# Zero products in sequence on one column strip, and a new order of the start, in a gated mix of two attention branches

## The chip, the cores and the metric

One core of a Trainium2 chip runs the kernel. The metric is the device time of one execution in microseconds; of the kernel before there are three timed runs, and the median counts. The engines are TensorE (matrix products), VectorE, ScalarE, GpSimd and SyncE (it only issues DMAs here); in the views of the profile they are PE (PEld for its weight loads), DVE, ACT, POOL and SP. They run side by side, each through its own queue in order, and wait for each other through semaphores.

## What is computed

x is 1 x 2048 x 512. Two attention branches with 32 heads of 16 read it: full attention (A), and local attention over 8 positions with a step of 2 (B). A gate per row mixes them.

```python
g = _sigmoid((x * gate_w).sum(-1, keepdims=True))
# A: qkv = x @ A_wqkv, per head of 16:
scores = einsum("bhqd,bhkd->bhqk", q, k) * Dh ** -0.5
o = einsum("bhqk,bhkd->bhqd", softmax(scores), v)      # then @ A_wo
# B: the same with 8 keys a row, idx = pos - 2 * [0..7], masked below 0, then @ B_wo
return g * a + (1 - g) * b
```

## The kernel before

Branch A makes the exponentials of 32 heads x 2048 x 2048 scores. The work is cut into **periods**: a chunk of 512 queries and a group of 4 heads (32 periods). A period has 64 **units**, each one head and one tile of 128 keys, so 128 x 512 scores. TensorE multiplies a unit's keys with the chunk's queries (`qk`, L815, tile `ring`), ScalarE takes the exponential (`ex`, L821, tile `pT`), TensorE multiplies it with the values and adds to the period's accumulator (`pv`, L834, tile `acc`). Units go in **sets** of three and two in turn, over two score buffers (`rA`, `rB`) with three `pT` buffers each. The last few units of a period have their exponential made on VectorE by a polynomial (`d_group`, L855: tiles `misc`, `dt`, `dg`, `pd`). The four heads of a group use the four column strips of TensorE's array (32 columns each); products on different strips run together.

A row's scores are shifted ahead of the exponential by a bound: the largest key entry (`kmax`) of a head times the absolute values of the query. For that a group's keys are copied to SBUF with a constant row (`kc`, L443, tile `kt_all`), their largest absolute value is reduced (`km`, L447), the maxima go into `selk_all` (L455), and a period's query projection (`q_proj`, L513) is followed by its copy (`qc`), its absolute value (`ab`), a product with `selk_all` (`bd`) and a sum (`ev`). Only then can the period's scores start.

At the start, x (four chunks of 512 rows) and the weights are loaded by SyncE (L380 to L388), TensorE transposes each chunk in two halves into the PSUM tile `pxt` (`tr`, L402), ScalarE copies the first half to `xT` and VectorE the second (`ev`, L412). Group 0's keys and values are projected, and the first query. Twelve products of constants (`warm`, L391) come first on TensorE.

Branch B (`b_tile`, L610) projects a tile of 128 rows, writes keys and values to DRAM, reads them back shifted, and GpSimd multiplies and adds; 16 tiles, one each 46.7 us from `b_start` in the plan.

The order is that of a **list scheduler** in the kernel's Python (`list_schedule`, L79). Every piece of work is an `Op` with an engine, an estimated duration, a due time, what it depends on and the buffers (`Tok`) it takes. The scheduler simulates the five engines with these estimates, always starts the due-first piece that can start, and the instructions are emitted in the order of the simulated times; each engine runs its own in that order. `S0` (L285) holds the planned start of each period, from `T0` (L265) at 0.457 us a unit. PSUM's `misc` tiles (two) serve all projections, `acc` (one) the accumulator.

The scheduler also keeps TensorE busy: a `pv` step may be preceded by **zero products** (`z32` times `ones_t`, added to the running accumulator, so they change nothing). Before the change a step gets four of them, one for each strip whose accumulation is open (L148 and L835), when the products counted in the last 3.2 us are under 20, or under 12 where the four would make the next scores late:

```python
            if o.fill and have < (DENSE_MIN if w is None or t + occ + FILL <= w[1] else DENSE_LOW):
                o.filled = True
                occ, lat, n = occ + FILL, lat + FILL, n + 4
```

In this count score products have no weight, and each value product counts one.

Of the kernel before, what the change touches and what calls it, by code (L numbers as in the profile page):

```python
# [21 lines left out]
    b_start=32.0,  # L22
# [34 lines left out]
class Op:  # L57

    def __init__(self, eng, occ, fn, dl, deps=(), alloc=(), use=(), lat=None, rel=0.0, name="",
                 dense=0, fill=False, after=(), cls="a"):  # L60
        self.eng, self.occ, self.fn, self.dl, self.rel, self.name = eng, occ, fn, dl, rel, name
        self.dense, self.fill, self.filled = dense, fill, False
# [4 lines left out]
        self.cls, self.clock = cls, False  # L67
# [4 lines left out]
QK_LEAD, LATE, DENSE_LOW = 0.6, 1.0, 12  # L72
LAT = dict(pe=0.25, dve=0.10, act=0.22, pool=2.5, sp=2.2)
DENSE_SPAN, DENSE_MIN, FILL = 3.2, 20, 0.35
# [4 lines left out]
def list_schedule(ops):  # L79
# [48 lines left out]
    while len(out) < len(ops):  # L128
# [19 lines left out]
        if o.dense:  # L148
            recent = [(tr, n) for tr, n in recent if tr > t - DENSE_SPAN]
            n = o.dense  # L150
            have = sum(x[1] for x in recent) + n
            if o.fill and have < (DENSE_MIN if w is None or t + occ + FILL <= w[1] else DENSE_LOW):
                o.filled = True
                occ, lat, n = occ + FILL, lat + FILL, n + 4
            recent.append((t, n))
# [17 lines left out]
def kernel(  # L173
# [91 lines left out]
    T0 = 22.0  # L265
# [51 lines left out]

    def init_dve():
        V.memset(ones_t[:], 1.0)
# [8 lines left out]
        V.memset(z32[:], 0.0)  # L328
# [13 lines left out]
    o_init_d = op("dve", 2.2, init_dve, -9.0)  # L342
# [37 lines left out]
    o_x[0] = op("sp", 0.5, load_x(0), -9.0, alloc=[xtok[0]], lat=5.5)  # L380
    o_wk = op("sp", 0.5, load_w(1), -8.9, lat=6.5)
    o_x[1] = op("sp", 0.5, load_x(1), -8.8, alloc=[xtok[1]], lat=7.5)
    o_x[2] = op("sp", 0.5, load_x(2), -8.7, alloc=[xtok[2]], lat=9.5)
    o_wq = op("sp", 0.5, load_w(0), -8.6, lat=11.0)
    o_x[3] = op("sp", 0.5, load_x(3), -8.5, alloc=[xtok[3]], lat=12.0)
    o_wv = op("sp", 0.5, load_w(2), -8.4, lat=13.0)
    o_bw = op("sp", 1.0, load_bw, -8.3, lat=19.0)
    o_wo = op("sp", 3.5, load_wo, -8.2, deps=[o_wz], lat=24.0)  # L388


    def warm():  # L391
        t_ = misc_ps([128, QW])
        for _ in range(3):
            mm_ct(t_, selq[:], ones_t[:], True, True)
    o_warm = op("pe", 4.0, warm, -9.0, deps=[o_init_d], alloc=[tok("misc", 2)])

    o_xt = []
    for sc in range(NC):
# [22 lines left out]
        t1 = op("pe", 0.6, tr(0), -5.0 + sc, deps=[o_x[sc], o_id], alloc=[tk], use=[xtok[sc]])  # L421
        t2 = op("pe", 0.6, tr(1), -4.9 + sc, deps=[t1], use=[tk, xtok[sc]])
        o_xt.append([op("act", 1.0, ev(0), -5.0 + sc, deps=[t1], use=[tk]),
                     op("dve", 0.68, ev(1), -4.9 + sc, deps=[t2], use=[tk])])
    all_xt = [o for os_ in o_xt for o in os_]


    o_kc = {}
    o_selk = {}

    def k_proj(i, sc, tag, dl, rel=0.0):
# [657 lines left out]
```

## Time and profile before

| what | us |
|---|---|
| median of 3 runs (941.53 to 947.1) | 944.49 |
| the profiled execution | 943.72 |
| its span, first to last instruction | 941.8 |
| first exponential on ScalarE | 25.58 |
| exponentials over 1536 columns, 386, each | 1.57 |
| exponentials over 1024 columns, 387, each | 1.14 |
| zero products, 974, on TensorE | 110.3 busy |

Rows of the profile's groups give engine, operation, what it writes and reads, busy time and mean duration. A product of 512 columns shows some 0.38 us, but products follow each other closer than that, since they are pipelined; so the length of a run of products is read from the timeline, and a busy TensorE is not one at its peak. Lines of a helper stand for many callers here (L230 for all of VectorE, ScalarE, GpSimd and SyncE, L239 for most products), so one goes by the tiles' names. The mean granted clock of TensorE is 0.989.

### The profile page before, as it was taken

What the parts mean: (1) busy time and instruction counts of PE and PEld (TensorE: products, weight loads), DVE (VectorE), ACT (ScalarE), POOL (GpSimd) and SP (SyncE); (2) the same over time, 40 slices, a digit from 0 to 9 for tenths busy, and PEclk for the clock granted to TensorE, in tenths of its full rate; (3) what the DMA queues carried; (4) which work ended last, traced back from release to release, by engine and by line L of the source; (5) the groups of instructions that cost most, each with busy time, mean ns of one, the idle gap of its engine ahead of it and who ended that gap; (6) DMA issues with size and microseconds to landing.
All of it is one profiled execution on the core that took longest, in us unless ns stands there. A gap on an engine that the chain in (4) does not pass through costs nothing.

```text
span 941.8 us, 20153 instructions
## 1 busy us (share of the span) xinstructions
PE 824.4 (88%) x8427; PEld 269.6 (29%) x8427; DVE 703.5 (75%) x877; ACT 888.9 (94%) x795; POOL 709.9 (75%) x540
## 2 busy tenths in 40 slices
PE   7999998888998889988999888888988888788997
PEld 4323233222332323222233222222222222222222
DVE  5587768768687788986253776978888698896776
ACT  2999999999999999999998999989999999899894
POOL 2355969598796999898969894999999999980000
PEclk9999999999999999999999999989999899999999
DMA  9301110203030112013030221130303010100001
GB/s 268 103 2 57 45 58 1 102 1 102 1 102 1 57 46 78 25 57 101 18 108 18 67 68 44 33 101 1 82 21 102 1 46 1 46 1 1 1 6 42
DMA packets 43940, 47.48 MB, mean 50 GB/s; under 512 B 1813, under 2 KB 41285, under 8 KB 43849
## 3 DMA queue, kind: packets, MB, share of 16 engines
q1 hardware_dynamic: 43848, 46.19, 15.5%
q8 instruction: 66, 1.08, 0.5%
q14 instruction: 26, 0.20, 0.1%
HBM read 39.86 MB, written 6.33 MB: 49 GB/s over the span
## 4 chain that ended last, share of the span: by engine, by line
ACT 43%; issue 19%; DVE 19%; PE 14%; POOL 4%; DMA 1%; SPq 0%; DVEq 0%; ACTq 0%; POOLq 0%
ACT pT L230 42%; DVE dg L230 6%; PE acc L239 5%; PE ring L239 4%; POOL prod L230 4%; DVE pd L230 4%; PE misc_ps L239 3%; DVE dt L230 1%; DVE kt_all L230 1%; DVE qt L230 1%; PE misc L239 1%; DVE kmax_all L230 1%; DVE accT L230 1%; DVE ott L230 1%; DVE lg L230 1%
## 5 line engine op out<-in xcount | busy, mean ns | idle before, releaser
L230 ACT ACTIVATE pT<-ring 128x1536 bf16<-128x1536 f32 (+1 forms) x773 | 881.8, 1355 | 25.3 <-PE ring L239 17.4
L239 PE MATMUL ring<-qt,kt_all 32*128 32x512 bf16 x1932 | 307.8, 383 | 82.5 <-ACT pT L230 76.1
L239 PE MATMUL acc<-pT,vp_all 128*17 128x512 bf16 (+1 forms) x1932 | 295.6, 386 | 5.4 <-DVE accT L230 5.2
L230 POOL TENSOR_TENSOR prod<-prod 128x512 f32<-128x512 f32 (+1 forms) x208 | 292.9, 1420 | 6.3
L230 POOL TENSOR_TENSOR prod<-ksh,qb 128x512 f32<-128x512 bf16 x128 | 179.8, 1434 | 71.8 <-issue 39.1
L239 PEld LDWEIGHTS <-kt_all 32*128 32x128 bf16 x2048 | 115.5, 91 | 398.4 <-issue 391.5
L230 POOL TENSOR_TENSOR prod<-vsh,lg 128x512 f32<-128x512 bf16 x128 | 162.9, 1302 | 51.8 <-DVE lg L230 30.5
L230 DVE TENSOR_SCALAR dt<-misc 128x512 f32<-128x512 f32 x116 | 79.7, 687 | 64.8 <-PE misc L239 57.6
L230 DVE SCALAR_TENSOR_TENSOR dg<-dt,dg 128x1024 bf16<-128x1024 uint16 x65 | 110.0, 1693 | 1.8
L239 PE MATMUL acc<-ones_t,z 128*32 128x512 bf16 x974 | 110.3, 393 | 0.0
L230 DVE SCALAR_TENSOR_TENSOR pd<-dg,dt 128x1024 uint16<-128x1024 bf16 x65 | 105.3, 1620 | 1.1
L239 PEld LDWEIGHTS <-vp_all 128*17 128x17 bf16 (+1 forms) x1932 | 70.0, 89 | 100.2 <-issue 90.7
L230 DVE SCALAR_TENSOR_TENSOR dg<-dt 128x1024 bf16<-128x1024 uint16 x65 | 93.6, 1440 | 1.8
L239 PE MATMUL misc_ps<-xT,wst 128*32 128x512 bf16 x1024 | 93.3, 389 | 0.4 <-DVE dt L230 0.3
L239 PE MATMUL misc_ps<-bw,xT 128*32 128x512 bf16 x768 | 69.0, 382 | 0.2 <-DVE vp_all L230 0.2
L239 PE MATMUL misc<-qt,kt_all 32*128 32x512 bf16 x116 | 44.5, 383 | 2.9 <-DVE dt L230 1.4
L239 PE MATMUL misc_ps<-woarr,oat 128*32 128x512 bf16 x512 | 43.7, 382 | 1.0 <-DVE fb L230 0.8
L239 PEld LDWEIGHTS <-z 128*32 128x32 bf16 x974 | 27.1, 93 | 58.1 <-issue 57.1
L239 PEld LDWEIGHTS <-xT 128*32 128x32 bf16 (+1 forms) x1088 | 33.7, 96 | 26.0 <-issue 17.8
L230 DVE CAST kvs<-misc_ps 128x512 bf16<-128x512 f32 x32 | 21.8, 682 | 21.6 <-PE misc_ps L239 21.5
L230 DVE TENSOR_SCALAR kt_all<-misc_ps,rowc 128x512 bf16<-128x512 f32 x32 | 25.6, 801 | 16.4 <-PE misc_ps L239 16.4
L239 PE MATMUL acc<-pd,vd_all 128*17 128x512 bf16 x116 | 28.0, 390 | 9.0 <-DVE pd L230 8.4
(71 smaller groups left out, 524.6 us busy)
## 6 DMA issues: line engine op xcount, KB each, us to landing
ksh<-kv_scr SPq DMA_DIRECT2D x16, 1024.0 KB, 6.2
vsh<-kv_scr SPq DMA_DIRECT2D x16, 1024.0 KB, 9.1
kv_scr<-kvs SPq DMA_DIRECT2D x16, 256.0 KB, 2.0
xld<-in_A_x_dram SPq DMA_DIRECT2D x4, 512.0 KB, 4.9
out_dram<-osb SPq DMA_DIRECT2D x16, 128.0 KB, 1.8
wst<-in_A_wqkv_dram SPq DMA_DIRECT2D x3, 512.0 KB, 4.9
bw<-in_B_wqkv_dram SPq DMA_DIRECT2D x1, 1536.0 KB, 10.2
bwo<-in_B_wo_dram SPq DMA_DIRECT2D x1, 512.0 KB, 14.1
```

Of the source, the lines that this page charges most:

```text
L230: return chain_on(key, f(*a, **k))
L239: return chain(nc.tensor.matmul(out, lhsT=lhsT, rhs=rhs, start=start, stop=stop, **kw))
```

## The change

- **Start.** x's fourth chunk is loaded ahead of the query weights. The two halves of a chunk's transposes follow each other (`after` orders two pieces by their start, without waiting for the end). TensorE's first products are seven on one strip, `z32` times `ones_t`, behind a step with only those two memsets, and one more behind chunk 0's transposes. Group 0's keys are copied by ScalarE (`kc_act`) while VectorE reduces their maxima, now from the PSUM tile itself. Group 0's values are projected after the first query's `bd`. Due times and planned durations of these steps change, and `T0` and `b_start` are earlier.
- **Zero products.** The scheduler counts passes of TensorE: a projection step of eight products two, a value step one, a score step 0.75. Where fewer than 8.6 lie in the last 3.4 us, one or two zero products go ahead of a value step, in sequence on one strip that this step uses (floor 6.8 where they would make scores late). Where TensorE is planned idle for over 0.5 us and the count is low, further ones are put into the gap (`pre`).

```diff
-    b_start=32.0,
+    b_start=26.0,
...
-QK_LEAD, LATE, DENSE_LOW = 0.6, 1.0, 12
+QK_LEAD, LATE, ACTIVE_LOW, GAP_MIN = 0.6, 1.0, 6.8, 0.5
 LAT = dict(pe=0.25, dve=0.10, act=0.22, pool=2.5, sp=2.2)
-DENSE_SPAN, DENSE_MIN, FILL = 3.2, 20, 0.35
+SPAN, ACTIVE, FILL, FILL1 = 3.4, 8.6, 0.25, 0.10
...
-        if o.dense:
-            recent = [(tr, n) for tr, n in recent if tr > t - DENSE_SPAN]
+        if e == "pe":
+            recent = [(tr, n) for tr, n in recent if tr > t - SPAN]
+            act = sum(n for tr, n in recent)
+            idle = t - free[e]
+            if t > 30.0 and idle > GAP_MIN and act < ACTIVE:
+                o.pre = min(int((idle - 0.1) / FILL), int(ACTIVE - act + 1))
+                recent.append((t - 0.1, o.pre))
+                act += o.pre
             n = o.dense
-            have = sum(x[1] for x in recent) + n
-            if o.fill and have < (DENSE_MIN if w is None or t + occ + FILL <= w[1] else DENSE_LOW):
-                o.filled = True
-                occ, lat, n = occ + FILL, lat + FILL, n + 4
+            if o.fill and act + n < ACTIVE:
+                for k in (2, 1):
+                    more = FILL1 + k * FILL
+                    if act + n + k - 1 < ACTIVE and (w is None or t + occ + more <= w[1] or act + n + k - 1 < ACTIVE_LOW):
+                        o.filled = k
+                        occ, lat, n = occ + more, lat + more, n + k
+                        break
...
-    T0 = 22.0
+    T0 = 19.0
...
+    def init_warm():
+        V.memset(z32[:], 0.0)
+        V.memset(ones_t[:], 1.0)
...
-    o_init_d = op("dve", 2.2, init_dve, -9.0)
+    o_init_w = op("dve", 0.6, init_warm, -9.5)
+    o_init_d = op("dve", 1.8, init_dve, -9.0, deps=[o_init_w])
...
-    o_x[0] = op("sp", 0.5, load_x(0), -9.0, alloc=[xtok[0]], lat=5.5)
-    o_wk = op("sp", 0.5, load_w(1), -8.9, lat=6.5)
-    o_x[1] = op("sp", 0.5, load_x(1), -8.8, alloc=[xtok[1]], lat=7.5)
-    o_x[2] = op("sp", 0.5, load_x(2), -8.7, alloc=[xtok[2]], lat=9.5)
-    o_wq = op("sp", 0.5, load_w(0), -8.6, lat=11.0)
-    o_x[3] = op("sp", 0.5, load_x(3), -8.5, alloc=[xtok[3]], lat=12.0)
-    o_wv = op("sp", 0.5, load_w(2), -8.4, lat=13.0)
-    o_bw = op("sp", 1.0, load_bw, -8.3, lat=19.0)
-    o_wo = op("sp", 3.5, load_wo, -8.2, deps=[o_wz], lat=24.0)
-
-
-    def warm():
-        t_ = misc_ps([128, QW])
-        for _ in range(3):
-            mm_ct(t_, selq[:], ones_t[:], True, True)
-    o_warm = op("pe", 4.0, warm, -9.0, deps=[o_init_d], alloc=[tok("misc", 2)])
+    o_x[0] = op("sp", 0.5, load_x(0), -9.0, alloc=[xtok[0]], lat=4.7)
+    o_wk = op("sp", 0.5, load_w(1), -8.9, lat=5.7)
+    o_x[1] = op("sp", 0.5, load_x(1), -8.8, alloc=[xtok[1]], lat=6.7)
+    o_x[2] = op("sp", 0.5, load_x(2), -8.7, alloc=[xtok[2]], lat=7.7)
+    o_x[3] = op("sp", 0.5, load_x(3), -8.6, alloc=[xtok[3]], lat=8.7)
+    o_wq = op("sp", 0.5, load_w(0), -8.5, lat=9.6)
+    o_wv = op("sp", 0.5, load_w(2), -8.4, lat=10.6)
+    o_bw = op("sp", 1.0, load_bw, -8.3, lat=14.5)
+    o_wo = op("sp", 3.5, load_wo, -8.2, deps=[o_wz], lat=17.0)
+
+
+    def warm(n):
+        def s():
+            t_ = misc_ps([128, QW])
+            for _ in range(n):
+                mm(t_[0:32, :], z32[:], ones_t[:], True, True, tile_position=(0, 0))
+        return s
+    op("pe", 3.2, warm(7), -30.0, deps=[o_init_w], alloc=[tok("misc", 2)])
...
-        t1 = op("pe", 0.6, tr(0), -5.0 + sc, deps=[o_x[sc], o_id], alloc=[tk], use=[xtok[sc]])
-        t2 = op("pe", 0.6, tr(1), -4.9 + sc, deps=[t1], use=[tk, xtok[sc]])
-        o_xt.append([op("act", 1.0, ev(0), -5.0 + sc, deps=[t1], use=[tk]),
-                     op("dve", 0.68, ev(1), -4.9 + sc, deps=[t2], use=[tk])])
+        if sc == 1:
+            op("pe", 0.45, warm(1), -21.0, after=[t2], alloc=[tok("misc", 2)])
+        t1 = op("pe", 0.57 if sc else 1.0, tr(0), -20.0 + sc, deps=[o_x[sc], o_id], alloc=[tk], use=[xtok[sc]])
+        t2 = op("pe", 0.57 if sc else 1.0, tr(1), -19.9 + sc, after=[t1], use=[tk, xtok[sc]])
+        o_xt.append([op("act", 1.0, ev(0), -20.0 + sc, deps=[t1], use=[tk]),
+                     op("dve", 0.68, ev(1), -19.9 + sc, deps=[t2], use=[tk])])
...
+        def kc_act():
+            A.activation(out=kt_all[:, i, sc * QW:(sc + 1) * QW], in_=st["pk"][:], func=ACT.Identity,
+                         scale=rowc[:, 0:1], bias=rowc[:, 1:2])
+
         def km():
-            V.tensor_reduce(out=kmax_all[:, i, sc:sc + 1], in_=kt_all[:, i, sc * QW:(sc + 1) * QW],
-                            axis=AX.X, op=ALU.max, apply_absolute_value=True)
-        a = op("pe", WAVE(2), part(0, 2), dl - 2.6, dense=8, deps=[o_wk, o_init_d] + o_xt[sc], alloc=[tk], rel=rel, name=f"kp{i}.{sc}")
-        b = op("pe", WAVE(2), part(2, DC), dl - 2.0, dense=8, deps=[a], use=[tk])
-        c = op("dve", 0.71, kc, dl - 0.8, deps=[b], use=[tk])
+            src = kt_all[:, i, sc * QW:(sc + 1) * QW] if i else st["pk"][:]
+            V.tensor_reduce(out=kmax_all[:, i, sc:sc + 1], in_=src, axis=AX.X, op=ALU.max, apply_absolute_value=True)
+        if i == 0:
+            b = op("pe", 0.95, part(0, DC), dl, dense=4, deps=[o_wk, o_init_d] + o_xt[sc], alloc=[tk], name=f"kp0.{sc}")
+            o_kp0.append(b)
+            o_k0.append(op("act", 0.72, kc_act, dl, deps=[b], use=[tk]))
+            return op("dve", 0.70, km, dl, deps=[b], use=[tk])
+        a = op("pe", WAVE(2), part(0, 2), dl - 2.6, dense=2, deps=[o_wk, o_init_d] + o_xt[sc], alloc=[tk], rel=rel, name=f"kp{i}.{sc}")
+        b = op("pe", WAVE(2), part(2, DC), dl - 2.0, dense=2, deps=[a], use=[tk])
+        c = op("dve", 0.81, kc, dl - 0.8, deps=[b], use=[tk])
...
+                o_kc[i].append(k_proj(i, sc, "misc", -10.0 + sc))
             else:
-                o_kc[i].append(k_proj(i, sc, "misc", S0[CP * i] - 17.0 - 8.0 * (NC - 1 - sc), rel=S0[CP * i - CP] - 12.0 if i > 1 else 10.0))
-        selk(i, 2.0 if i == 0 else S0[CP * i] - 16.0)
+                o_kc[i].append(k_proj(i, sc, "misc", S0[CP * i] - 17.0 - 8.0 * (NC - 1 - sc), rel=S0[CP * i - CP] - 12.0 if i > 1 else 20.5))
+        selk(i, -0.5 if i == 0 else S0[CP * i] - 16.0)
...
-        a = op("pe", 0.62, mk(0), dl - 2.0, dense=8, deps=[o_wv] + xs, alloc=[tk], rel=rel, name=f"vp{h0}.{tb}")
-        b = op("pe", 0.62, mk(1), dl - 1.4, dense=8, deps=[a], use=[tk])
+        a = op("pe", 0.62, mk(0), dl - 2.0, dense=1, deps=[o_wv] + xs, alloc=[tk], rel=rel, after=[o_kp0[-1]] if h0 else [o_bd0[0]], name=f"vp{h0}.{tb}")
+        b = op("pe", 0.62, mk(1), dl - 1.4, dense=1, deps=[a], use=[tk])
...
-        a = op("pe", WAVE(2), part(0, 2), dl - 4.0, dense=8, deps=[o_wq, o_init_d] + o_xt[c_] + ([o_selk[i]] if pi else [o_kc[0][1]]), alloc=[tk, ta, tq], rel=rel, after=[last_q[0]], name=f"qp{pi}")
+        if pi == 0:
+            a = b = op("pe", 0.95, part(0, DC), -7.5, dense=4, deps=[o_wq, o_init_d] + o_xt[c_], alloc=[tk, ta, tq], name="qp0")
+        else:
+            a = op("pe", WAVE(2), part(0, 2), dl - 4.0, dense=2, deps=[o_wq] + o_xt[c_] + [o_selk[i]],
+                   alloc=[tk, ta, tq], rel=rel, after=[last_q[0]], name=f"qp{pi}")
+            b = op("pe", WAVE(2), part(2, DC), dl - 3.4, dense=2, deps=[a], use=[tk])
         last_q[0] = a
-        b = op("pe", WAVE(2), part(2, DC), dl - 3.4, dense=8, deps=[a], use=[tk])
-        c = op("dve", 0.70, qc, dl - 2.8, deps=[b], use=[tk, tq])
-        c = op("dve", 0.55, ab, dl - 2.4, deps=[c], use=[ta, tq])
-        d = op("pe", WAVE(1), bd, dl - 1.4, dense=4, deps=[c, o_selk[i]], use=[tk, ta])
+        c = op("dve", 0.82, qc, dl - 2.8, deps=[b], use=[tk, tq])
+        c = op("dve", 0.45, ab, dl - 2.4, deps=[c], use=[ta, tq])
+        d = op("pe", WAVE(1), bd, dl - 1.4, dense=1, deps=[c, o_selk[i]], use=[tk, ta])
+        o_bd0.append(d)
...
+    q_proj(0, "acc", -0.2)
+    v_proj(0, 4, 0, 8, "misc", 0.5)
+    v_proj(0, 4, 8, 8, "misc", 3.0)
+    for h0, h1, pn in ((4, 8, 1), (8, 16, 2), (16, 24, 4), (24, 32, 6)):
+        TB = 512 // ((h1 - h0) * DH)
+        for tb in range(0, NT, TB):
+            v_proj(h0, h1, tb, TB, "misc", S0[CP * pn] + tb * 1.3 - 4.0, rel=max(20.5, S0[CP * pn - CP] - 4.0))
     for pi in range(1, NP):
-        q_proj(pi, "misc", S0[pi] - 16.0, rel=S0[pi - 1] - 4.0)
+        q_proj(pi, "misc", S0[pi] - 16.0, rel=S0[pi - 1] + 4.0 if pi == 1 else S0[pi - 1] - 4.0)
...
+    def zeros(pi, n, first=()):
+
+        js = [j for j in list(first) + list(range(4)) if 1 <= todo[(pi, j)] < NT]
+        for k in range(n if js else 0):
+            j = js[0]
+            mm(acc_tiles[pi][32 * j:32 * j + 32, :], z32[:], ones_t[:], False, False, tile_position=(0, 32 * j))
...
-        kd = [o_kc[periods[pi][1]][t // TPC] for pi, t, j in us]
-        a = op("pe", 0.30 + 0.02 * n, qk, tn - 1000.0, deps=[o_q[pi] for pi in pis] + kd,
+        kd = [o_kc[periods[pi][1]][t // TPC] for pi, t, j in us] + [o_k0[t // TPC] for pi, t, j in us if periods[pi][1] == 0]
+        a = op("pe", 0.30 + 0.02 * n, qk, tn - 1000.0, dense=0.75, deps=[o_q[pi] for pi in pis] + kd,
...
-                if st["op", pi].filled:
-                    for j in range(4):
-                        if 1 <= todo[(pi, j)] < NT:
-                            mm(acc_tiles[pi][32 * j:32 * j + 32, :], z32[:], ones_t[:], False, False, tile_position=(0, 32 * j))
+                zeros(pi, st["op", pi].filled, [j for _, t, j in mine])
...
-            o = op("pe", 0.21, pv, tn - 2.0, dense=len(mine), fill=not first, deps=[b] + [o_v[(4 * periods[pi][1] + j, t)] for _, t, j in mine]
+            o = op("pe", 0.21, pv, tn - 2.0, dense=1, fill=not first, deps=[b] + [o_v[(4 * periods[pi][1] + j, t)] for _, t, j in mine]
...
+        if o.pre and acc_tiles:
+            zeros(max(acc_tiles), o.pre)
```

In the other steps only `dense`, the weight in this count, changes (8 products to 2, 4 to 1), and a few planned durations.

## The prediction

> **What bounds the kernel now.** First the page's busy times, then the stretches before, within and after the exponentials, then the timeline of the start, ScalarE's waits, and the granted clock around its falls.
>
> ```profile
> span 941.8 us, 20153 instructions
> ...
> PE 824.4 (88%) x8427; PEld 269.6 (29%) x8427; DVE 703.5 (75%) x877; ACT 888.9 (94%) x795; POOL 709.9 (75%) x540
> ```
>
> ```profile
> 25.58:928.65 903.07, 798.17 (x8075) 256.27 (x8075) 680.10 (x819) 883.56 (x790) 702.98 (x529) 0.99 0.14 45
> 928.65:941.80 13.15, 6.77 (x102) 2.66 (x99) 8.77 (x14) 0.00 (x0) 0.00 (x0) 0.85 0.19 61
> 0.00:25.58 25.58, 19.48 (x253) 10.70 (x253) 14.60 (x46) 5.33 (x5) 6.88 (x11) 1.00 0.88 249
> ```
>
> The second fence (after the bounds: length, then busy time of PE, weight load, DVE, ACT, POOL, granted clock, DMA) is the map. ScalarE is the bound between its first and last exponential: 883.56 busy of 903.07, so 19.51 idle. Before it, 25.58 us pass with 5.33 of ScalarE work; after it, 13.15 us of finishing. The time is start + exponentials + their idle time + end, and a change is worth what it takes from the first, third or fourth.
>
> ```profile
> 7.69 0.69 DVE L230 COPY xT<-pxt 128x1024 bf16<-128x1024 bf16 x1 [4.54 <-ACT xT L230]
> 8.73 1.04 PE L239 MATMUL misc_ps<-xT,wst 128*32 128x512 bf16 x8
> ...
> 20.95 0.61 PE L239 MATMUL misc_ps<-xT,wst 128*32 128x512 bf16 x8
> 21.09 0.29 DVE L230 TENSOR_SCALAR absq<-qt 128x512 uint16<-128x512 uint16 x1
> 21.30 0.68 DVE L230 TENSOR_REDUCE kmax_all<-kt_all 128x1 f32<-128x512 bf16 x1
> 21.90 0.80 DVE L230 TENSOR_SCALAR kt_all<-misc_ps,rowc 128x512 bf16<-128x512 f32 x1
> 22.73 0.69 DVE L230 TENSOR_REDUCE kmax_all<-kt_all 128x1 f32<-128x512 bf16 x1
> ...
> 25.58 1.45 ACT L230 ACTIVATE pT<-ring 128x1536 bf16<-128x1536 f32 x1 [8.01 <-PE ring L239]
> ```
>
> Three things in the start. ScalarE stands idle 8.01 us before its first exponential, while VectorE works through key copies (0.80 each) and key maxima (0.69 each) for four chunks: in the chain of waits the last 7 us are VectorE's, bar two short TensorE pieces. Eight projection products take 1.04 us early and 0.61 later, so TensorE is cold at first (in the clock's records full speed begins at 12.97). And VectorE's copy of a transposed chunk started 0.04 after ScalarE's copy from the same PSUM tile ended: two engines' reads of one PSUM tile go one after the other here.
>
> ```profile
> ACT pT L230 <- PE ring L239: 17.4, 21, 8.0
> ...
> ACT pT L230 <- PE acc L239: 7.2, 6, 2.6
> ACT lg L230 <- DVE lg L230: 2.2, 3, 1.3
> ```
>
> Less the 8.0 of the start, 18.8 of the 19.5 us are named: 9.4 for score products, 7.2 for the products with the values (the score buffers' release), 2.2 for VectorE.
>
> ```profile
> 620.54:623.95 3.41, 1.18 (x7) 0.28 (x7) 3.31 (x6) 3.41 (x4) 3.41 (x3) 1.00 0.92 287
> 623.95:627.37 3.42, 3.11 (x18) 0.68 (x17) 3.32 (x6) 3.04 (x4) 3.26 (x4) 0.50 0.89 299
> ...
> 729.77:733.18 3.41, 2.21 (x17) 0.59 (x16) 3.38 (x3) 3.01 (x4) 3.33 (x4) 1.00 0.00 0
> 733.18:736.59 3.41, 2.16 (x11) 0.42 (x9) 3.26 (x6) 2.54 (x3) 3.17 (x4) 0.50 0.00 0
> ...
> 815.10:818.51 3.41, 1.49 (x13) 0.51 (x8) 3.38 (x4) 2.12 (x4) 3.41 (x3) 1.00 0.48 161
> 818.51:821.93 3.42, 3.26 (x20) 0.69 (x19) 3.28 (x7) 3.26 (x3) 3.26 (x3) 0.50 0.41 146
> ```
>
> The clock falls to 0.50 three times inside the exponentials, each at the end of a 3.41 us stretch in which TensorE did little: 1.18, 2.21 and 1.49 us busy. ScalarE's gaps just in and behind these falls add up to 0.38+0.13+1.18, 0.40+0.87+0.66 and 0.69: **4.3 us**, the most that a steadier clock can give back. All three stretches lie where one accumulator ends and the next waits for VectorE's transpose (the timeline has 1.25 and 1.44 us of such a wait at 734.5 and 818.7).
>
> **The change, part by part.**
>
> *Loads.* The fourth x load goes past the query weights on SP's queue, one issue past one issue, 512 KB each. The first loads land at 4.67, 6.12 and 7.72 (issue plus time to landing), 1.5 us apiece. So x lands at 4.7, 7.7, 9.2 and 10.7, not 12.2 for the last; the query weights at 12.2, not 10.7. Nothing else on SP moves.
>
> *Warming.* Twelve products in three rounds, at 1.64 behind VectorE's memsets, become seven in sequence behind two memsets (0.07 + 0.48 from 0.91): cold passes of 0.43 (1.04 less 0.61 for eight products, two passes) from 1.5 to 4.5, then transposes from 4.7. The stretch before 12.97 had TensorE busy 3.29 of 3.42, and the cold one at 733.18, busy 2.16, did not bring the clock back. So the clock should rise when one of its 3.41 us stretches is nearly full. Work from 1.5 to 6.6 holds such a stretch for about two phases in three (a start within 1.5-0.3 to 6.6-3.1, 2.3 of 3.4). I take a warm clock from x's second chunk; otherwise it stays cold to about 12.97.
>
> The Trainium skill (TensorE: Matmul & The Clock Gate, Part 4: PE-mode transpose) says that transposes do not count as TensorE activity in the same way, which speaks against this step: seven passes of 0.43 are 3.0 us, under the window of about 3.4 us of the same page's Part 1. By it the clock would stay cold and the sum be that of the late-clock rival below; here the full stretch that ended at 12.97 had over 2 us of transposes in it, so I go by the row.
>
> *ScalarE's key copies.* Four copies of 128x512 from PSUM leave VectorE (4 x 0.80 = 3.2 us) and go into ScalarE's idle time. The trace has none of that form on ScalarE: under 1.01 (its 1024-column copy), over 0.5 (half of it); 0.7 taken. The maximum now reads the same PSUM tile, so by the 7.69 row copy and maximum go one after the other: 0.7 + 0.69 instead of 0.80 + 0.69, but on two engines. Behind a key copy in ScalarE's queue stand only x copies that are not due, and then the first exponential.
>
> *Value projection of group 0* moves behind the first query's bias product. It is covered by six buffers of exponentials (15 units, 1932 units in 883 us, so 0.457 each: 6.9 us); it needs 2 x (1.1 + 0.69), about 3.6. Without that cover each microsecond late would cost one.
>
> *The sum of the start*, with warm rows: 16 transposes 1.2 (two of 0.61), copies 1.01 then 0.69, 16 products 0.86 pitch (four passes of 0.216: 32 products took 1.91, eight 0.61). TensorE: chunk 1 transposed 7.75-8.95, keys 0 to 9.8, chunk 2 to 11.0, chunk 3 (landed 10.7) to 12.2, keys 1 and 2 to 13.9, query to 14.8, keys 3 once keys 1's bank is read, 14.8-15.65 and 0.2 to drain. VectorE: chunk 3's copy 13.3-14.0 behind ScalarE's, maxima 1 and 2 to 15.5 (each behind its key copy), query 0.80 and absolute value 0.29 to 16.6, maximum 3 to 17.3, its two small steps to 17.8; bias product 0.40, sum 0.69, scores 0.39 with their hand-overs: first exponential at **19.4**, a gain of 25.58 - 19.4 = **6.2 us**. Best case: behind x at 10.7 only transposes 1.2, copies 1.7, keys 1.05, maximum 0.69 and 2.2 to the scores: 17.6 (8.0 gained). Worst: cold rows add 0.7 and 1.0 before chunk 2 and 0.4 in it, 21.5 (4.1 gained).
>
> *Zero products.* Before: 974 in fours, some 244 passes of 0.216 = 53 us of TensorE. After: one or two passes in sequence on one strip, wherever the planner counts under 8.6 passes in 3.4 us, and into planned idle time over 0.5. Counted its way (773 score sets and 116 single scores at 0.75, 838 value steps, 672 projection passes and some 50 small steps) the other work is 2230 passes, 8.4 in 3.4 us, so gaps of a pass or two: I take 350 passes, 75 us; bounds 0 and two for each of 773 sets. They lie in the idle time that TensorE has while ScalarE holds both score buffers, and cost nothing unless scores come late; without that cover 0.216 each. Their good is bounded by 4.3; as all three falls lie where no accumulator is open, and zeros need an open one, I take **0**, with -4.3 and +4.3 as ends (none, or twice as many falls).
>
> *Else.* The local-attention branch starts 6 us earlier in the plan; GpSimd is idle in the last 90 us, so that is free. The end keeps 13.15. Planner durations change, so the order is drawn anew and the 14 us of idle that have nothing to do with the clock may come out a few us either way; 0 taken, 5 as an end.
>
> Sum: the profiled execution took 943.72 (span 941.8 and 1.9 around it), 0.8 under the median 944.49. 943.72 - 6.2 = **937.5**.
>
> **The rivals.**
> *Late clock* (0.17): TensorE stays cold to about 13 us, or the serial reads of one PSUM tile stretch the start; for it, the rise at 12.97 in spite of twelve warming products; against it, five unbroken us of TensorE work. 943.7 - 4.1 = 939.6, to 941.
> *Steadier clock* (0.13): the falls go too. For it, the clock fell after 2.21 us busy, so stretches near that tip either way and a pass more would hold them; against it, the closed accumulators. 937.5 - 4.3 = 933.2.
> *New order, new stalls* (0.09): the output projections ahead of the value products stalled ScalarE 1.88, 1.30 and 2.59 at 494, 504 and 878; as much again would give 937.5 + 5 = 942.5.
> *Slower* (0.09): passes in sequence keep the next score product waiting; score lateness is ScalarE's largest wait already (9.4). Each exposed pass costs 0.216. 29 of them eat the 6.2; past 54 of the 350, (949.2 - 937.5)/0.216, it is slower; at 60 it is 950.5. Against it, TensorE's idle time ahead of scores is mostly spent waiting for ScalarE (76 us in 241 waits).
>
> **The numbers.** Forecast 0.52 with its own range 935 to 940. A measurement tells apart about 0.5%: 939.8 and 949.2. Faster: nine tenths of the forecast, the steadier clock, a third of the late clock: 0.67; slower 0.09; same 0.24. The range reaches from a share of the steadier clock to new stalls: 932.5 to 944.
>
> **What would show it.** The first exponential near 19.4 (21 or later: late clock), VectorE's stretch before it without key copies, eight products at 0.61 by 9 us, the exponentials' stretch again about 903 with some 19.5 idle, and three falls or so. It is wrong if that stretch grows by more than 3, if scores make ScalarE wait more than 9.4, or if the end is not 13 us.

## The result

| | median, us | executions | ratio to the kernel before [95%] |
|---|---|---|---|
| kernel before | 948.14 (941.53 to 961.86) | 20 | 1 |
| changed kernel | 937.91 (930.86 to 947.82) | 20 | 0.9882 [0.9852, 0.9912] |

The change makes the kernel faster by 1.2%, about 11 us. Ratios leave out executions that took over 1.5% longer than the fastest of their kernel, and medians do not, so the two can differ where few executions were made (e9_start_order; for e10_after no ratio is left). The profiled execution of the changed kernel took 933.24 us. Its page first (busy time of each engine), and then the same three stretches as before (bounds, length, busy time of PE, weight load, DVE, ACT, POOL, granted clock, DMA):

```profile
span 931.5 us, 18744 instructions
...
PE 818.5 (88%) x7720; PEld 271.4 (29%) x7720; DVE 688.0 (74%) x873; ACT 890.5 (96%) x799; POOL 703.4 (76%) x540
```

```profile
0.00:21.28 21.28, 16.55 (x193) 9.41 (x193) 8.88 (x38) 8.12 (x10) 6.85 (x11) 1.00 0.96 289
21.28:919.41 898.13, 795.23 (x7428) 259.27 (x7428) 670.64 (x822) 882.34 (x790) 696.56 (x529) 0.98 0.15 45
919.41:931.50 12.09, 6.77 (x101) 2.69 (x99) 8.51 (x14) 0.00 (x1) 0.00 (x0) 0.90 0.20 67
```

Against the execution before, the start gives 25.58 - 21.28 = 4.3 us, the stretch of the exponentials 903.07 - 898.13 = 4.9, the end 13.15 - 12.09 = 1.1: 10.3 in all. In the stretch ScalarE's own work is about the same (883.56 and 882.34), and its idle time falls from 19.5 to 15.8. ScalarE's waits over the whole span (us in total, times, longest):

```profile
ACT pT L239 <- PE ring L248: 9.8, 16, 1.6
...
ACT pT L239 <- PE acc L248: 6.7, 5, 2.9
...
ACT lg L239 <- DVE lg L239: 0.2, 1, 0.2
```

Less the start's 1.6, scores cost 8.2 (9.4 before), the value products 6.7 (7.2) and VectorE 0.2 (2.2).

The timeline of the start shows where the first exponential's time goes (start, duration, engine, line, operation, in brackets the idle time ahead and what ended it):

```profile
8.00 1.89 PE L422 MATMUL pxt<-ident,xld 128*128 128x128 bf16 x16 [0.38 <-DMA xld<-in_A_x_dram]
...
9.82 1.52 PE L248 MATMUL misc_ps<-xT,wst 128*32 128x512 bf16 x16
...
11.58 0.68 DVE L239 TENSOR_REDUCE kmax_all<-misc_ps 128x1 f32<-128x512 f32 x1
12.29 0.78 ACT L239 ACTIVATE kt_all<-misc_ps,rowc 128x512 bf16<-128x512 f32 x1 [1.36 <-DVE kmax_all L239]
12.97 1.92 ACT L239 COPY xT<-pxt 128x1024 bf16<-128x1024 bf16 x2
...
15.53 1.28 DVE L239 TENSOR_REDUCE kmax_all<-misc_ps 128x1 f32<-128x512 f32 x2
16.24 1.45 ACT L239 ACTIVATE kt_all<-misc_ps,rowc 128x512 bf16<-128x512 f32 x2 [1.36 <-DVE kmax_all L239]
...
17.07 1.05 PE L248 MATMUL misc_ps<-xT,wst 128*32 128x512 bf16 x16 [0.84 <-ACT kt_all L239]
18.17 0.69 DVE L239 TENSOR_REDUCE kmax_all<-misc_ps 128x1 f32<-128x512 f32 x1 [0.64 <-PE misc_ps L248]
...
20.84 0.60 PE L248 MATMUL ring<-qt,kt_all 32*128 32x512 bf16 x5
21.28 1.45 ACT L239 ACTIVATE pT<-ring 128x1536 bf16<-128x1536 f32 x1 [1.61 <-PE ring L248]
```

Two things are to be seen. Chunk 1 is transposed cold, that is at half clock (1.89 us; chunk 0 took the same), and full speed begins at 10.82. And a key copy on ScalarE stands **behind** VectorE's maximum of the same PSUM tile (12.29 follows the end of 11.58), with x's chunk 2 behind it in ScalarE's queue, whose transposes were ready: ScalarE waits 1.36 us, TensorE waits 0.84 for the copy before it can write keys 3 (17.07), and the last maximum starts at 18.17.

### The profile page after: what moved, and what is told of

It is laid out like the page before. It is cut to its first block, busy times and chain, and to the rows that moved or that the text cites. A ratio compares the mean times of both kernels' runs of the same rounds, so it can differ in the third digit from the quotient of the medians.

```text
span 931.5 us, 18744 instructions
## 1 busy us (share of the span) xinstructions
PE 818.5 (88%) x7720; PEld 271.4 (29%) x7720; DVE 688.0 (74%) x873; ACT 890.5 (96%) x799; POOL 703.4 (76%) x540
## 4 chain that ended last, share of the span: by engine, by line
ACT 58%; issue 21%; PE 14%; DVE 5%; DMA 1%; SPq 0%; DVEq 0%; ACTq 0%
ACT pT L239 57%; PE ring L248 5%; PE misc_ps L248 4%; PE acc L248 4%; DVE dg L239 2%; ACT lg L239 1%; DMA xld<-in_A_x_dram 1%; PE misc L248 1%; DVE pd L239 1%; DVE osb L239 0%; ACT xT L239 0%; DVE dt L239 0%; DVE qt L239 0%; DVE kmax_all L239 0%; PE pxt L422 0%
## 5 line engine op out<-in xcount | busy, mean ns | idle before, releaser
L248 PE MATMUL acc<-pT,vp_all 128*17 128x512 bf16 (+1 forms) x1932 | 317.1, 390 | 1.8 <-DVE accT L239 1.5
L239 POOL TENSOR_TENSOR prod<-prod 128x512 f32<-128x512 f32 (+1 forms) x208 | 284.0, 1377 | 6.3
L239 DVE SCALAR_TENSOR_TENSOR dg<-dt,dg 128x1024 bf16<-128x1024 uint16 x65 | 106.3, 1636 | 1.6
L239 DVE SCALAR_TENSOR_TENSOR pd<-dg,dt 128x1024 uint16<-128x1024 bf16 x65 | 100.5, 1546 | 6.9 <-PE acc L248 5.7
L248 PE MATMUL misc_ps<-xT,wst 128*32 128x512 bf16 x1024 | 98.2, 390 | 1.0 <-ACT kt_all L239 0.8
L248 PE MATMUL acc<-ones_t,z 128*32 128x512 bf16 x271 | 95.1, 390 | 0.0
L248 PE MATMUL misc_ps<-bw,xT 128*32 128x512 bf16 x768 | 71.8, 385 | 0.6 <-DVE kvs L239 0.6
L239 DVE STREAM_TRANSPOSE accT<-acc 128x512 f32<-128x512 f32 x32 | 22.8, 712 | 17.3 <-PE acc L248 17.1
L239 DVE TENSOR_SCALAR kt_all<-misc_ps,rowc 128x512 bf16<-128x512 f32 x28 | 22.5, 802 | 17.3 <-PE misc_ps L248 17.3
L239 DVE TENSOR_TENSOR qt<-qt,misc_ps 128x512 bf16<-128x512 bf16 x32 | 21.8, 682 | 17.3 <-PE misc_ps L248 17.1
## 6 DMA issues: line engine op xcount, KB each, us to landing
bwo<-in_B_wo_dram SPq DMA_DIRECT2D x1, 512.0 KB, 13.8
```

The lines of the kernel that those rows point to most:

```text
L239: return chain_on(key, f(*a, **k))
L248: return chain(nc.tensor.matmul(out, lhsT=lhsT, rhs=rhs, start=start, stop=stop, **kw))
```

## Time against the granted clock

Executions of one kernel differ by 17 us (changed) and 20 us (before), and nearly all of it goes with the clock. Each execution is listed with its mean granted clock. A straight line through the 26 executions of the changed kernel (with the six of e10_after below) falls 5.4 us per 0.01 of clock and leaves a scatter of 1.1 us; one through 62 of the kernel before falls 5.0 and leaves 1.5. Read at a clock of 0.985, the lines give 946.0 before and 933.3 changed: **12.7 us at an equal clock**. The mean clocks are 0.976 and 0.975, so the change has not made the clock steadier. Such a line shows that time and clock go together, not which of them moves the other: a stall of TensorE also lets the clock fall. Where a kernel's time is given below "at 0.985", it is read from such a line through its own executions.

## The experiments

The first two runs take the change apart: its start with the old zero rule, and its zero rule with the old start.

**e1_before.** The kernel before, unchanged, as a yardstick.

> The kernel before, unchanged, to see how its time goes with the mean granted clock over many executions. Theory (the changed kernel is not helped by a steadier clock): its mean granted clock is 0.97 to 0.99 as in the changed kernel (0.959 to 0.988), and at the same clock it is some 10 us longer. Rival (the zero products in sequence hold the clock better): its mean clock is lower by 0.01 or more, and at the same clock the two kernels differ only by the 4.3 us of the start.

Measured: 946.77 us (12 executions), ratio 0.9988 [0.9959, 1.0018]. Its profiled execution repeats the one shown: first exponential at 25.86, stretch 904.8, idle 21.0, end 12.9. The theory held: the two kernels' mean clocks are alike, and the gap at an equal clock stays (section above).

**e2_start_only.** The changed start and plan, the old zero rule.

```diff
+            have = sum(x[1] for x in recent) + n
+            if o.fill and have < (DENSE_MIN if w is None or t + occ + FILL <= w[1] else DENSE_LOW):
+                o.filled = True
+                occ, lat, n = occ + FILL, lat + FILL, n + 4
...
-                zeros(pi, st["op", pi].filled, [j for _, t, j in mine])
+                        if 1 <= todo[(pi, j)] < NT:
+                            mm(acc_tiles[pi][32 * j:32 * j + 32, :], z32[:], ones_t[:], False, False, tile_position=(0, 32 * j))
```

> The changed kernel with the old rule for zero products (four at once, counted by instructions, none in planned gaps); the start, the loads, ScalarE's key copies and all planned times are the new ones. Theory (the gain is the start, 4.3 us, and some 5 us of fewer stalls that come with the new plan and not with the zeros): 937 to 940, ratio 0.989 to 0.992. Rival (the zeros are worth what the start does not explain): only the start is left, some 944, ratio 0.995.

Measured: 962.47 us (6), ratio 1.0120 [1.0085, 1.0155]: slower than before, and outside what either theory expected. The first exponential came at 23.23 (full speed began at 6.52 and was lost again from 9.93 to 13.35 and from 20.17 to 23.59), and the stretch grew to 921.8 with 36.4 idle, of which 23.3 have nothing to do with the clock (15.5 before). ScalarE's waits for scores and value products:

```profile
ACT pT L230 <- PE ring L239: 26.6, 34, 2.8
ACT pT L230 <- PE acc L239: 11.4, 7, 4.2
```

So 18 us came from somewhere that is neither the start nor the zeros' form; the next pair of runs asks where.

**e3_zeros_only.** The kernel before with the new zero rule and its pass counts.

```diff
-DENSE_SPAN, DENSE_MIN, FILL = 3.2, 20, 0.35
+SPAN, ACTIVE, FILL, FILL1, ACTIVE_LOW, GAP_MIN = 3.4, 8.6, 0.25, 0.10, 6.8, 0.5
...
+                zeros(pi, st["op", pi].filled, [j for _, t, j in mine])
```

> The kernel before with the new rule for zero products alone (counted in passes, in sequence on one strip, also into planned gaps); start and planned times are the old ones. Theory: no gain, ratio 0.997 to 1.003, first exponential at 25.6. Rival (the zeros give about 5 us): ratio 0.993 to 0.996 with the first exponential still at 25.6.

Measured: 951.71 us (12), ratio 1.0010 [0.9983, 1.0037]. The new zero rule alone brings nothing, in the draw that it gives. The profiled execution was 41 us cold within the exponentials, the one before 17.

**e7_after_b32 and e8_start_b32.** One constant of the plan, set back in the changed kernel and in e2_start_only; it says when the local-attention tiles are due, and through the planner it draws the order of everything anew. (A draw is below the order that the planner happens to emit for one set of times.)

```diff
-    b_start=26.0,
+    b_start=32.0,
```

> The changed kernel with the planned start of the local branch back at 32 instead of 26, nothing else. Theory (every change of the plan draws the order of the exponentials' stretch anew, and the draws differ by some us whatever was changed): 3 us or more away from the changed kernel, most likely slower, 941 to 950, with other places of ScalarE's gaps. Rival (the new rule for zeros with the new start is good in itself): within 2 us, 936 to 940.

> The new start with the old rule for zeros, as in the run of the start alone, but with the local branch's planned start at 32. Theory (the 962 of that run was one draw of the order): 5 us or more away from 962, 940 to 955. Rival (the old rule cannot hold the clock with the new start): again 957 or more, mean clock 0.97 or less.

Measured: e7 958.19 us (6), ratio 1.0100 [1.0049, 1.0152]; e8 946.97 (12), ratio 0.9982 [0.9947, 1.0017]; e7 lost more than its theory had, e8 came as its theory had it. The constant alone moves the changed kernel by 20 us one way and the start-only kernel by 15 the other way. Together with the runs above (medians, us):

| | old zeros, b_start 32 | old zeros, 26 | new zeros, 32 | new zeros, 26 |
|---|---|---|---|---|
| old start | 946.8 to 950.7 | not run | 951.7 | not run |
| new start | 947.0 | 962.5 | 958.2 | **937.9** |

No column and no row of it holds a steady gain or loss. The six kernels share their arithmetic and nearly all their work, and lie 25 us apart. e8 is the plainest: its first exponential came at 21.06, 4.5 us before that of the kernel before, and its median is the same. What a draw costs can go in good part through the clock, as in e7's page (forty slices of the span, in tenths of full speed):

```profile
PEclk9999999999999799999999999789958799979999
```

In e7's profiled execution 106 us of the stretch ran at half clock (27 in the changed kernel), and its idle time is 38.7 us (15.8); only 13.8 of that lies outside the cold stretches (10.5). In e2 it was the other way round: 23.3 lay outside.

**e4_no_zeros.** The changed kernel without any zero product behind the start. The planner then counts no time for them, so this is a new draw as well: VectorE's order parts from the changed kernel's at 75 us (in e5, e6, e9, e11 and e12 it is the same to the end).

```diff
-            if t > 30.0 and idle > GAP_MIN and act < ACTIVE:
+            if False:
...
-            if o.fill and act + n < ACTIVE:
+            if False:
```

> The changed kernel without any zero products behind its start: what they are worth at all. Theory (the clock falls after stretches with about 1.5 us of passes or less, and each us at half speed costs about 0.3): many more stretches fall, mean clock 0.90 or less, 15 to 40 us slower than the changed kernel, 953 to 978, ratio over 1.005. Rival (TensorE has room enough even when slow; the zeros are worth little): within 3 us of the changed kernel, ratio about 0.99.

Measured: 984.64 us (6), ratio 1.0356 [1.0320, 1.0392], mean clock of the profiled execution 0.842. Its page has the clock in forty slices again:

```profile
PEclk9999999779998999997999968577865656656899
```

307 us of the stretch ran at half clock (27 in the changed kernel), and ScalarE's idle time grew from 15.8 to 54.4, of it 45.2 in or just behind the cold stretches. The two kernels lie 984.6 - 937.9 = 47 us apart, more than the theory's 15 to 40; how much of it is the draw was not measured, but the lost time is cold time. That zeros cost anything can't be seen: 10.5 us of idle time lie outside the cold stretches in the changed kernel, 9.2 here.

**e6_four_strips and e11_four_strips.** The changed kernel with its planned order kept; each zero pass goes to all strips whose accumulation is open (as before the change), not to one. The two runs are the same kernel; e10_after repeats the changed kernel beside the second.

```diff
-        for k in range(n if js else 0):
-            j = js[0]
+        for j in [j for _ in range(n) for j in range(4) if 1 <= todo[(pi, j)] < NT]:
```

> The changed kernel's order and number of zero passes, but each pass on all open strips at once (four products instead of one), as in the kernel before. Theory (only passes count, for the clock and for the time): within 2 us of the changed kernel, 936 to 940, ratio 0.987 to 0.991. Rival (the form counts: fewer instructions on TensorE, or a strip in use): 3 us or more away from it, ratio over 0.992, or a mean clock away by over 0.01.

> Each zero pass on all open strips at once in the changed kernel's order, again, beside the changed kernel itself. Theory (only passes count; 932.5 in the first look was chance and that chip): within 2.5 us of the changed kernel of this group. Rival (passes in sequence on a strip in use cost time or clock): 4 to 6 us faster than it again, ratio 0.980 to 0.983.

> The changed kernel, unchanged, on the same chip as the other two of this group: 935 to 940, ratio 0.985 to 0.991; first exponential between 21.0 and 22.0, about 11 us of ScalarE's idle time outside the clock's falls.

Measured: e6 932.52 us (6), ratio 0.9807 [0.9761, 0.9854]; e11 935.58 (6), ratio 0.9846 [0.9799, 0.9893]; e10 945.12 (6: 939.57, 945.54, 947.72, 944.69, 946.94, 930.55), above the 935 to 940 expected of it. All executions taken together, four strips have a mean of 934.0 (12) and the changed kernel 938.8 (26): 4.9 us less, with a 95% interval of 1.9 to 7.7; over the executions that ratios count (12 and 20) it is 2.5 us, -0.2 to 5.2. So a gain is likely and its size open. Their cold time within the exponentials was 17 and 8 us, in the changed kernel 27 and 48, and at 0.985 eleven of their executions (without the odd one of the last section) come to 935.2, not below the changed kernel's 933.3: what they gain goes with the clock. A likely reason is in the count of passes. Products that start within 100 ns of each other on different strips run in one pass. The trace of the changed kernel has 271 zero products; 120 of them have a pass to themselves, and 151 start together with value products of other strips and so add no time in which TensorE is busy. With four strips there are 990 zero products in some 340 passes, and 261 of these hold zeros alone. The part of the change that its name speaks of, the sequence on one strip, thus seems to give some of the clock away; no run held the number of passes equal in the two forms.

**e5_more_warm.** The changed kernel with more warming: eight passes ahead of x, not seven, and two behind chunk 0, not one.

```diff
-    op("pe", 3.2, warm(7), -30.0, deps=[o_init_w], alloc=[tok("misc", 2)])
+    op("pe", 3.2, warm(8), -30.0, deps=[o_init_w], alloc=[tok("misc", 2)])
...
-            op("pe", 0.45, warm(1), -21.0, after=[t2], alloc=[tok("misc", 2)])
+            op("pe", 0.45, warm(2), -21.0, after=[t2], alloc=[tok("misc", 2)])
```

> The changed kernel with eight instead of seven warming products and two instead of one behind chunk 0's transposes; every other instruction and the whole order stay. Theory (the start's missing 1.9 us are the late clock: x's second chunk was still transposed cold, in 1.89 us): the clock rises by 8 us in more executions, chunk 1 is transposed in 1.2, the first exponential comes at 20.0 to 20.6 instead of 21.28, time 1 us less, ratio 0.987. Rival (the chain from chunk 1 on waits for ScalarE's and VectorE's turns at PSUM anyway): first exponential at 21.0 to 21.4 also with a warm chunk 1.

Measured: 939.80 us (6), ratio 0.9874 [0.9819, 0.9928], no different from the changed kernel; the first exponential, at 21.66, lies nearer the rival's range than the theory's. The timeline:

```profile
8.23 1.07 PE L422 MATMUL pxt<-ident,xld 128*128 128x128 bf16 x16 [1.23 <-DMA xld<-in_A_x_dram]
9.23 1.05 PE L248 MATMUL misc_ps<-xT,wst 128*32 128x512 bf16 x16
...
17.58 0.69 DVE L239 TENSOR_REDUCE kmax_all<-misc_ps 128x1 f32<-128x512 f32 x1 [0.64 <-PE misc_ps L248]
...
19.21 1.86 PE L248 MATMUL misc_ps<-wst,xT 128*128 128x64 bf16 x32
...
21.00 1.03 PE L248 MATMUL ring<-qt,kt_all 32*128 32x512 bf16 x5
21.66 1.45 ACT L239 ACTIVATE pT<-ring 128x1536 bf16<-128x1536 f32 x1 [2.57 <-PE ring L248]
```

Chunk 1 is now warm (1.07 and 1.05), and the last maximum starts at 17.58, only 0.6 earlier than in the changed kernel. Then TensorE waits for VectorE, the clock falls from 19.29 to 22.70, the value projection takes 1.86 and holds up the scores, and the gain is gone.

**e9_start_order.** The changed kernel with the key copies of chunks 0 to 2 emitted ahead of their maxima, and group 0's value projection behind the first two further sets of scores. Everything else keeps its order.

```diff
+    for sc in range(NC - 1):
+        if at(f"km0.{sc}") < at(f"kc0.{sc}"):
+            o = order.pop(at(f"kc0.{sc}"))
+            order.insert(at(f"km0.{sc}"), o)
+    for tb, behind in ((0, "qk1"), (8, "qk2")):
+        names = [n + f"0.{tb}" for n in ("vp", "vb", "vc")]
+        got = [order.pop(at(n)) for n in names]
+        k = at(behind) + 1
+        order[k:k] = got
```

> The changed kernel with two moves in its start and the same order elsewhere: ScalarE's key copies of chunks 0 to 2 go ahead of VectorE's maxima of the same PSUM tile instead of behind them, and group 0's value projection goes behind the first two (and the third) score sets instead of ahead of them. Theory (what the start still lacks lies in these two turns, not in loads or the clock alone): x's third and fourth chunks are copied 0.7 us earlier on ScalarE, scores follow the query's sum at once, first exponential at 19.6 to 20.5 instead of 21.28, time 1 us less than the changed kernel. Rival (VectorE's own chain of copies and maxima sets it): first exponential at 20.8 or later.

Measured: 940.25 us (6: 930.83, 945.19, 927.88, 942.48, 938.01, 945.86), ratio 0.9809 [0.9742, 0.9876]. Its timeline:

```profile
8.04 1.07 PE L422 MATMUL pxt<-ident,xld 128*128 128x128 bf16 x16 [1.61 <-DMA xld<-in_A_x_dram]
...
10.14 0.78 ACT L239 ACTIVATE kt_all<-misc_ps,rowc 128x512 bf16<-128x512 f32 x1
...
10.95 0.69 DVE L239 TENSOR_REDUCE kmax_all<-misc_ps 128x1 f32<-128x512 f32 x1
11.12 2.02 ACT L239 COPY xT<-pxt 128x1024 bf16<-128x1024 bf16 x2 [0.20 <-PE pxt L422]
...
16.12 0.68 DVE L239 TENSOR_REDUCE kmax_all<-misc_ps 128x1 f32<-128x512 f32 x1
...
19.08 2.37 ACT L239 ACTIVATE pT<-ring 128x1536 bf16<-128x1536 f32 x2 [1.47 <-PE ring L248]
```

The key copy now waits for nothing (10.14), x's chunk 2 follows at once, and the last maximum starts at 16.12. With chunk 1 warm in both, that is 1.5 us before e5 (17.58), which in turn was 0.6 before the changed kernel: of the 2.05 us between 18.17 and 16.12, the order of copy and maximum holds 1.5 and the cold chunk 0.6 (1.3 and 0.8 when counted from chunk 1's first transpose, which came at 8.04 here and at 8.23 in e5). The moved value projection took some of the gain back: it ran cold behind the first scores (1.89 us at 19.36), and ScalarE waited 0.39 and 0.67 for the next ones; in e12, with the same order and a warm clock, it did not. In the time itself 2.2 us cannot be told from the clock's scatter: the means over all executions are 938.4 (6) and 938.8 (26); at 0.985 it is 931.8 against 933.3.

**e12_fill_start.** The three edits together: e9's order, four strips, and more filling in the start.

```diff
-    op("pe", 3.2, warm(7), -30.0, deps=[o_init_w], alloc=[tok("misc", 2)])
+    op("pe", 3.2, warm(8), -30.0, deps=[o_init_w], alloc=[tok("misc", 2)])
...
-            op("pe", 0.45, warm(1), -21.0, after=[t2], alloc=[tok("misc", 2)])
+            op("pe", 0.45, warm(4), -21.0, after=[t2], alloc=[tok("misc", 2)])
...
+    order.insert(at("kp0.3") + 1, op("pe", 1.1, warm(5, "rA"), 0.0))
```

> The changed kernel with three edits at once: the order of the start as in e9_start_order, the zero passes on all open strips as in e6_four_strips, and more filling passes in the start (8 warming passes, not 7; 4 behind chunk 0's transposes, not 1; 5 behind group 0's last key projection). The planned order of everything else is the same. Theory (the start's loss was the hand-overs of the key copies plus a clock that fell in TensorE's waits; both are mended): the clock, once up, stays up from about 8 us into the exponentials, the first exponential starts at 18.4 to 19.4 and not at 21.3 to 23.7, the stretch keeps the 895 to 897 us of the four-strip runs: a profiled span of 926 to 929 us, a median of 929 to 933, ratio 0.977 to 0.984. Rival (the gains don't add up, the clock still falls while x's second chunk is awaited, or the added passes delay chunk 1 and the scores): first exponential at 20.5 or later, median 934 to 937 as four strips alone.

Measured: 937.03 us (6: 926.65, 939.71, 927.29, 943.33, 941.13, 934.35), ratio 0.9844 [0.9787, 0.9901]. The profiled execution is the shortest of the study. Its three stretches:

```profile
0.00:19.23 19.23, 15.83 (x170) 8.46 (x170) 9.07 (x38) 8.40 (x10) 6.85 (x11) 1.00 0.95 306
19.23:912.95 893.72, 794.38 (x8179) 263.52 (x8179) 672.98 (x822) 881.47 (x790) 699.55 (x529) 1.00 0.15 46
912.95:924.88 11.93, 6.76 (x101) 2.70 (x99) 8.51 (x14) 0.00 (x1) 0.00 (x0) 0.99 0.20 68
```

The start is as the theory had it (19.23), and the clock fell once, for 3.41 us, in the whole stretch. But that is one execution: over six, the mean is 935.4 against 934.0 for four strips alone, and the median lies on the rival's side. That the three gains add up is not shown. The only version for which the runs point to a time below that of the changed kernel is the one with four strips.

## Why the prediction came out, step by step

The forecast was 937.5 us, the measured median 937.91. The sum is right, but not by its own terms: it took 6.2 us from the start and nothing elsewhere, off a median of 944.49, while the kernel before came out at 948.14 over 20 executions and the gain is about 11. That it lands 0.4 us from the median is in part luck: a start 1.9 us short was more than made up by 4.9 us in the stretch and 1.1 at the end, and the reference was 3.6 too low.

- **What bounds the kernel** (ScalarE, with start, idle time and end around it): held. ScalarE's work stayed within 1.2 us, and all the rest lies in the three terms named.
- **The start, 6.2 us: too large; 4.3.** The end of the loads' chain was right (x landed at 5.1 and 7.9; forecast 4.7 and 7.7). "I take a warm clock from x's second chunk" was wrong in the profiled execution and right in others: full speed began at 10.82 there, at 5.18 in e9 and 6.49 in e12, and in e10 it began at 4.52 and was lost from 7.93 to 11.34, while TensorE waited for chunk 1. Where it falls depends on how the clock's stretches lie to the program's start. In the nine profiled executions with seven warming products it came by 6.7 us in six, which is the forecast's two phases in three; but in four of the six it was lost again 3.4 us later, and that the forecast did not have. The rival *late clock* had the time of the first exponential (21.5; 21.28 to 21.87 in the profiled executions of the changed kernel, e4, e5, e6 and e10, 23.66 in e11), but in the execution shown the clock accounts for only 0.6 to 0.8 of the missing 1.9.
- **The step that failed** is "maxima 1 and 2 to 15.5 (each behind its key copy)", and with it "behind a key copy in ScalarE's queue stand only x copies that are not due". Two readers of one PSUM tile do go one after the other, as the row of before showed; but which goes first is the planner's choice, and it put the maximum first. So the key copy was late and what stood behind it in ScalarE's queue, x's chunk 2, was due. Price: 1.3 to 1.5 us (e9 against e5). With copy and maximum in the forecast's order and chunk 1 warm, the first exponential came at 19.08 (e9) and 19.23 (e12), against 19.4 in the sum. The copy itself took 0.78, within the bounds 0.5 to 1.01 (0.7 taken).
- **Group 0's value projection, covered by six buffers: nearly.** The buffers covered the values. But the projection was put ahead of the scores on TensorE; it delayed them by 0.2 when warm (query sum done at 20.61, scores at 20.84), and by more when cold (e5).
- **Zero products, 0 against the old rule: held** (e3: ratio 1.0010), with 271 of them and not 350. Three falls in the stretch became four. "Cost nothing unless scores come late" fits too (10.5 us of idle time outside cold stretches with them, 9.2 in e4). What the bounds missed is how much zeros are worth at all (some 47 us, e4, draw included), since the trace of before shows the clock with them alone; and that a zero product on one strip often shares its pass, so that the number of zeros is not the number of added passes.
- **"The order is drawn anew ... 0 taken, 5 as an end": the mis-sized term.** In the changed kernel the draw was lucky: idle time outside cold stretches fell from 15.5 to 10.5 us, a value that the profiled executions with this order repeat (10.5 to 13.0 in the changed kernel, e5, e6, e9, e10, e11 and e12). In e2 the same term was 23.3. The end drawn for it, 5, was right in size for this draw, and its sign was open; e2 and e7, 15 and 20 us above the same kernels with the other `b_start`, show that a draw can cost three to four times that on the bad side once the clock falls in its wake.
- **The end keeps 13.15: off by 1.1.** 12.09, and 11.8 to 12.2 in each profiled execution with this order and its zeros, but also 12.2 in e7, another draw. So the draw alone does not make it, and which piece does is not shown.
- **Steadier clock**: did not come about (0.975 and 0.976). **Slower by passes in sequence**: did not come about as a delay of scores (8.2 of waits against 9.4); what the sequence seems to cost is clock, which four strips held better.
- **A chance**: by its own terms the chance of "faster" is 0.66 (0.47 + 0.13 + 0.06), not 0.67.

Not settled: which of the many moved pieces makes one draw stall less than another. The runs point to the order rather than to the two mechanisms; they give no rule for it, and since `b_start` also shifts the local branch's own work, they don't part the order from that shift.

## What to carry to other kernels

When a hand-made planner fixes the order, any edit of a due time or a duration draws a new order, and that may move more than the edit itself: here 15 to 20 us for one constant, against 4.3 for the new start. Judge an idea at a fixed order (edit what is emitted, as in e6 and e9, not what the planner counts, as in e3 and e4), and search over the plan's constants separately. Where two engines read one PSUM tile, write down which of them goes first, and give the first turn to the one with due work queued behind it.

## What the runs showed of the hardware

- **The clock falls by pass time.** Its events lie on a grid of 3.413 us (143.36 us from the rise at 10.82 to the first fall is 42 of them). A pass is counted here as its columns at full speed (512 columns, 0.213 us), and products on different strips at the same time as one pass. Over the 14 profiled executions, within the exponentials: of 53 grid stretches at full clock in which TensorE's passes filled less than 0.43, 52 were followed by a fall; of 142 between 0.43 and 0.50, 29; of 244 between 0.50 and 0.55, 3; of 3050 above, none. In the start it is less sharp: stretches filled to 0.38, 0.41 and 0.42 (e6 at 16.2 us, e8 at 6.7, e9 at 5.2) kept the clock. The used share of the array (rows times columns of each product's tile) separates less well: of 590 stretches with a share from 0.20 to 0.30, 46 fell. The Trainium skill (TensorE: Matmul & The Clock Gate, Part 1: The HAM clock gate) has the free-running window of 3413 ns, which these events agree with, and lets the clock go cold after an idle window; here it fell in stretches that were more than a third busy. The four falls of the changed kernel's stretch came behind stretches filled to 0.38, 0.45, 0.41 and 0.52. The profile's busy time overstates this, as a stretch and the cold one behind it show (TensorE's busy time comes first after the length, the granted clock third from the end):

```profile
533.06:536.48 3.42, 2.24 (x21) 0.60 (x20) 3.38 (x2) 3.42 (x5) 3.42 (x3) 1.00 0.50 147
536.48:539.89 3.41, 3.22 (x15) 0.77 (x14) 3.27 (x7) 2.87 (x4) 3.33 (x3) 0.50 0.62 212
```

- **Transposes count for the rise.** In the changed kernel the stretch that ended with the rise at 10.82 held 1.9 us of transposes and 1.0 of products. The cold stretch at 733.18 in the kernel before, with TensorE busy 2.16 us, stayed cold, so the 1.0 us alone would hardly have done it. The same page's Part 4 (PE-mode transpose), which the prediction weighed, says that transposes do not count in the same way; in this row they counted enough to bring the full clock.
- **A microsecond at half clock goes with 0.17 to 0.29 us more time here.** By the lines, 0.01 of mean clock is 18.6 us at half clock in 931 and goes with 5.0 to 5.4, so 0.27 to 0.29; by e4, 280 more us at half clock and 47 us more time, 0.17, though in another draw.
- **One execution was granted 0.949 as its full clock** (e6, every event but the cold ones), with 932.55 us no slower than its neighbours.
